# LayerNorm, gated FFN and sliding-window attention on one core: weights in pieces of 128 rows with row halves that swap column blocks, and a first chunk whose first 256 rows go through on their own

## The chip, the core and the metric

The kernel runs on one core of a Trainium2 chip. Its engines work side by side and meet through semaphores only: TensorE (PE; its weight loads are listed apart as PEld), VectorE (DVE), ScalarE (ACT), GpSimd (POOL) and SyncE (SP), the last of which here only starts transfers. Transfers are started from the queues of SP, POOL and, once, ACT, and are carried by 16 DMA engines. Matmul results land in PSUM, eight banks of 512 float32 columns per partition; everything else lies in SBUF, 128 partitions wide.

The metric is device time in microseconds (us), the median of several runs. Before the change: 560.89 us (three runs, 560.74 to 561.54).

## The reference

```python
def reference(x, k_cache, v_cache, wq, wo, B_x, w_gate, w_up, w_down):
    # x (1, 2048, 448); Hq 16 query heads, Hkv 8 key heads, Dh 256; W = 512 last keys
    xn = layernorm(x)                                   # no scale, no bias
    q = (xn @ wq)                                       # 448 x 4096
    p = softmax(q @ k[:, last W].T * Dh**-0.5)          # per head, no mask
    s = (p @ v[:, last W]) @ wo                         # 4096 x 448
    g = silu((gelu(xn @ w_gate) * (xn @ w_up)) @ w_down)  # 448 x 1792 twice, 1792 x 448
    return x + s * g
```

All tensors are bfloat16. `B_x` is not used: both branches take `x`.

## The kernel before

**Recording.** `Rec.op` (L65) records one operation for one engine with the keys that it reads (`r`) and writes (`w`). From the keys it derives what the operation waits for, other engines' operations and transfers. An operation of an engine does not wait for an earlier one of the same engine where the engine's order is enough, and TensorE never waits for itself. `emit` (L98) writes out each engine's list in the recorded order, so the order of the calls in the code is the order in each engine's queue. A wait is placed ahead of the first instruction of an operation, and holds up all that is recorded behind it on that engine.

**Tiling.** The 2048 rows are four chunks (`c`) of 512 rows, each of four tiles (`t`) of 128. The model width of 448 is 7 pieces (`NK`) of 64 (`HP`). Since a piece has 64 rows of contraction, TensorE's 128 rows are used as two halves: one matmul in partitions 0 to 63 and one in 64 to 127 run side by side, each writing its own PSUM bank. `xnT` holds the transposed normalized rows, each piece twice, in both halves of the partitions. In `wgu` the gate weights lie in the lower half and the up weights in the upper half; in `wq` the even heads lie in the lower half and the odd heads in the upper one.

**Start.** `x0` loads the four tiles of chunk 0 on SP's queue, then come the gate and up weights in four slices (`load_gu`, cut at blocks 2, 6 and 10), the rows of chunk 1, `wd`, and the rows of chunks 2 and 3. Chunk 0 is normalized by VectorE (`ln_stats`, `ln_norm`; ScalarE gives the square root), two tiles at a time, and transposed on TensorE (`ln_tr`, 14 matmuls per tile); ScalarE and VectorE copy two tiles each from PSUM. `warm` runs 12 matmuls on zeros before that.

**FFN.** For each chunk, `gate_up(c, f)` runs over 14 blocks (`f`) of 128 FFN columns: 14 matmuls of 512 columns in 7 pairs, gate into bank `s`, up into bank `s + 1`, where the bank pair rotates over three (banks 0 to 5). ScalarE applies GELU to the gate bank (L374), VectorE multiplies it with the up bank (L376) into `actT`. While this goes on, `ln_later` and `ln_later2` normalize the next chunk's tiles: statistics on VectorE, reciprocal square root on POOL (L345, L347), two normalized copies on VectorE (L294), and a transposing transfer on SP's queue (L236). For chunk 0 this begins at block 4 (`lead`), for the others at block 1. `down` (L382) multiplies `actT` with `wd`, four tiles of 14 matmuls of 448 columns, in banks 6 and 7. `load_piece` sends off `wq`, `V` and `wo` in pieces on POOL's queue between these steps.

**Attention.** The last chunk's `down` is not run at its place but cut up as filling (`fill`) for the first slots of attention. The main loop runs over 64 heads-times-chunks (`i`) and four row tiles (`t`), one slot each: `scores` (L420) in bank 4 or 5, exponential on ScalarE (L424) into one of nine buffers `pr`, division on VectorE (L426, L427), transposing transfer into `pT`; `values` (L440) of an earlier head in every second slot, copied out by VectorE (L446); half of an output projection (L460) in each odd slot from `i` = 6. After the values of slot (`i`, 0), with `i` = 3, 7, 11 and so on, `q_burst` computes the queries of the next four heads: four parts of 7 pairs (L406), each copied out by ScalarE over two banks (L410), in bank pairs 0 and 2 by turns; the first burst, after the FFN, uses 4, 0, 2, 0.

Of the kernel before, what the change touches and what calls it, by code (L numbers as in the profile page):

```python
# [11 lines left out]
P = 128  # L12
# [10 lines left out]
class Rec:  # L23
# [41 lines left out]
    def op(self, eng, fn, r=(), w=(), dma=False, after=(), lane=None):  # L65
# [17 lines left out]
        for d, raw in deps:  # L83
            if d.eng == eng and not d.dma and not dma and (eng == "tensor" or not raw and eng != "gpsimd"):
                continue
            d.inc = d.waited = True
            o.deps.append(d)
# [54 lines left out]
def bass_recurrent_scan__sliding_block_cached__geglu_ffn__prompt_kernel(nc, A_x, A_k, A_v, A_wq, A_wo, B_x, B_wg, B_wu, B_wd, out):  # L142
# [6 lines left out]
    QC, TPC, HP = 512, 4, 64  # L149
    NQC = S // QC  # L150
    NT = NQC * TPC
    NK = D // HP
    NF, NJ, NE = F // P, W // P, Dh // P
    assert S % QC == 0 and D % HP == 0 and NE == 2 and NJ == 4 and Hq == 2 * Hkv and Hq % 4 == 0 and NF % 2 == 0
# [4 lines left out]
    with es:  # L159
# [20 lines left out]
        xnT, _ = sb("xnT", [P, NQC, NK, QC], BF16)  # L180
# [3 lines left out]
        wq, _ = sb("wq", [P, NK, Hkv, Dh], BF16)  # L184
        wo, _ = sb("wo", [P, Hq * NE, D], BF16)
        gu_at = off[0]
        wgu, x_at = sb("wgu", [P, NK, F], BF16)
        x4, _ = sb("x4", [P, NT, D], BF16)
        NX = 4
        xn2, d_at = sb("xn2", [P, NX, NK, 2, HP], BF16)  # L190
        wd, _ = sb("wd", [P, NF, D], BF16)
        actT, hb_at = sb("actT", [P, NF, QC], BF16)
        NHB = 4
        hb, ffn_end = sb("hb", [P, NHB, QC], BF16)

# [9 lines left out]
        while at + 2 * W <= d_at:  # L205
            t_, at = sb("pr%d" % len(pr), [P, W], BF16, at)
            pr.append(t_)
        at = hb_at
        while at + 2 * W <= ffn_end:
            t_, at = sb("pr%d" % len(pr), [P, W], BF16, at)  # L210
            pr.append(t_)
# [27 lines left out]
        dve(lambda e: e.memset(actT[:, NF - 1, :], 0.0), w=[("actT", NF - 1)])  # L239
# [9 lines left out]
        wg_v = B_wg.rearrange("(k p) f -> p k f", p=HP)  # L249
        wu_v = B_wu.rearrange("(k p) f -> p k f", p=HP)  # L250
        cuts = [0, 2, 6, 10, NF]
        fslice = {f: s for s in range(4) for f in range(cuts[s], cuts[s + 1])}

        def load_gu(s):
            a, b = cuts[s] * P, cuts[s + 1] * P
            dma("sync", wgu[0:HP, :, a:b], wg_v[:, :, a:b], w=[("wgu", 0, s)])
            dma("sync", wgu[HP:P, :, a:b], wu_v[:, :, a:b], w=[("wgu", 1, s)])
# [6 lines left out]
        for sl in range(4):  # L264
# [4 lines left out]
        for c in range(2, NQC):  # L269
# [5 lines left out]
        wq_v = A_wq.rearrange("(k p) (g two m) -> p k g two m", p=HP, two=2, m=Dh)  # L275
        pieces = [(wq[lo * HP:(lo + 1) * HP, k, :, :], wq_v[:, k, :, lo, :], ("wq", lo, k))
                  for k in range(NK) for lo in range(2)]
# [312 lines left out]
```

## Time and profile before

| what | value |
|---|---|
| median of three runs | 560.89 us |
| the profiled execution | 561.18 us |
| its span, first to last instruction | 559.4 us |
| granted TensorE clock, mean | 1.000 |
| chunk 0 gate and up, first to last matmul | 9.26 to 30.98 us |
| gate and up of one later chunk, by the chain of waits | 21.26 us |
| `down` of one chunk, by the chain of waits | 10.70 us |
| first query burst; the later ones | 6.04 us; 6.15 us |
| one period of four heads with its burst (251.15 to 277.27) | 26.12 us |
| up weights of slice 0 / 1: issue, to landing | 3.36, 4.3 us / 4.70, 7.8 us |
| `wq` pieces, issue to landing, shortest / median / longest | 3.5 / 4.3 / 6.7 us |

How to read it: busy time of an engine is a share of the span; "idle before, releaser" at the end of a group says how long the engine stood still before these instructions and what ended it. A line such as `9.26 3.20 PE L370 ... x28` in the timeline gives start, length, engine, line of the code and how many instructions are merged. The chain of waits is the work that ended last, followed back from the end of the program. In a table by stretches, each engine has its busy time and number of instructions, and the last three columns are the granted clock, the busy share of the DMA engines and GB/s.

### The profile page before, as it was taken

How to read it: one execution, taken by the hardware profiler on the slowest of the kernel's cores; microseconds unless marked ns; L12 is line 12 of the kernel's file. 1: busy time of each engine (PE TensorE's matmuls, PEld its weight loads, DVE VectorE, ACT ScalarE, POOL GpSimd, SP SyncE). 2: the span in 40 equal slices, each digit the busy share in tenths (PEclk: the TensorE clock that was granted, in tenths of full speed). 3: DMA queues.
4: the chain of work that ended last, by engine and by line, in shares of the span. 5: the costliest groups of instructions: out<-in, count | busy, mean ns of one | idle time of the engine just before them, and what ended most of it. 6: DMA issues, size and time to landing. Idle time of an engine off the chain costs nothing.

```text
span 559.4 us, 9865 instructions
## 1 busy us (share of the span) xinstructions
PE 549.0 (98%) x3499; PEld 257.2 (46%) x3532; DVE 322.9 (58%) x835; ACT 296.1 (53%) x673; POOL 90.1 (16%) x125
## 2 busy tenths in 40 slices
PE   7999999999999999999999999999999999999997
PEld 3544444444444444444444444444444444444445
DVE  5636446143464847474846657484747484755674
ACT  4324233247655565556565656656565656565641
POOL 0232323200000111013501101232100021400023
PEclk9999999999999999999999999999999999999999
DMA  8994746972453435353664344445535353645352
GB/s 193 276 191 86 138 102 136 247 137 65 94 85 68 97 64 99 69 91 64 143 98 94 73 86 71 81 84 137 101 67 99 63 95 71 147 79 101 70 92 52
DMA packets 169552, 58.83 MB, mean 105 GB/s; under 512 B 160160, under 2 KB 166432, under 8 KB 169504
## 3 DMA queue, kind: packets, MB, share of 16 engines
q1 hardware_dynamic: 166208, 45.50, 44.2%
q0 software_dynamic: 3152, 12.65, 8.9%
q8 instruction: 28, 0.46, 0.4%
q14 instruction: 20, 0.16, 0.1%
q10 hardware_dynamic: 144, 0.06, 0.0%
HBM read 17.92 MB, written 1.84 MB: 35 GB/s over the span
## 4 chain that ended last, share of the span: by engine, by line
PE 95%; DMA 1%; DVE 1%; issue 1%; SPq 1%; ACT 0%
PE ps L440 20%; PE ps L420 19%; PE ps L406 18%; PE ps L460 16%; PE ps L370 15%; PE ps L382 8%; DMA wgu<-in_B_w_up_dram 1%; SPq L233 1%; DVE tmp L469 0%; DVE ofin L471 0%; DVE pr L427 0%; DVE oT L446 0%; DVE rden L426 0%; ACT pr L424 0%
## 5 line engine op out<-in xcount | busy, mean ns | idle before, releaser
L424 ACT ACTIVATE pr<-ps 128x512 bf16<-128x512 f32 x256 | 152.8, 597 | 116.6 <-PE ps L420 112.5
L420 PE MATMUL ps<-kT,qT 128*128 128x512 bf16 x481 | 145.4, 379 | 3.3 <-issue 2.5
L440 PE MATMUL ps<-pT,V 128*128 128x512 bf16 x510 | 130.8, 379 | 0.6 <-DVE rden L426 0.4
L426 DVE RECIPROCAL rden<-den 128x1 f32<-128x1 f32 x256 | 41.5, 162 | 152.4 <-ACT pr L424 134.3
L460 PE MATMUL ps<-wo,oT 128*128 128x448 bf16 (+1 forms) x536 | 116.3, 344 | 0.0
L427 DVE TENSOR_SCALAR pr<-pr,rden 128x512 bf16<-128x512 bf16 x256 | 106.4, 416 | 9.0
L406 PE MATMUL ps<-xnT,wq 64*128 64x512 bf16 x896 | 99.5, 376 | 0.0
L410 ACT ACTIVATE qT<-ps 128x1024 bf16<-128x1024 f32 x64 | 65.5, 1024 | 49.8 <-PE ps L406 49.8
L370 PE MATMUL ps<-xnT,wgu 64*128 64x512 bf16 x784 | 85.5, 376 | 1.0 <-ACT xnT L322 0.8
L446 DVE CAST oT<-ps 128x512 bf16<-128x512 f32 x124 | 84.6, 682 | 0.6 <-PE ps L440 0.5
L440 PEld LDWEIGHTS ps<-pT,V 128*128 128x128 bf16 x512 | 49.9, 98 | 60.8 <-issue 1.2
L460 PEld LDWEIGHTS ps<-wo,oT 128*128 128x128 bf16 x536 | 52.3, 98 | 51.1
L420 PEld LDWEIGHTS ps<-kT,qT 128*128 128x128 bf16 x512 | 48.5, 98 | 57.1 <-issue 7.3
L376 DVE TENSOR_TENSOR actT<-ps,hb 128x512 bf16<-128x512 f32 x56 | 38.1, 685 | 57.5 <-ACT hb L374 55.7
L406 PEld LDWEIGHTS ps<-xnT,wq 64*128 64x128 bf16 x896 | 42.4, 94 | 55.9 <-DVE acc L481 4.2
L374 ACT ACTIVATE hb<-ps 128x512 bf16<-128x512 f32 x56 | 33.4, 597 | 51.8 <-PE ps L370 51.8
L370 PEld LDWEIGHTS ps<-xnT,wgu 64*128 64x128 bf16 x784 | 39.2, 94 | 46.5 <-issue 2.5
L424 ACT ACTIVATION_READ_ACCUMULATOR pr<-ps 128x1 f32 x256 | 49.9, 195 | 0.0
L500 POOL TENSOR_SCALAR tmp<-tmp 128x448 f32<-128x448 f32 x16 | 9.1, 572 | 233.9 <-ACT tmp L499 233.9
L382 PE MATMUL ps<-wd,actT 128*128 128x448 bf16 x224 | 46.2, 353 | 0.1
L485 POOL TENSOR_TENSOR tmp<-acc,gy 128x448 f32<-128x448 f32 x16 | 16.6, 1035 | 123.2 <-DVE acc L481 123.2
L382 PEld LDWEIGHTS ps<-wd,actT 128*128 128x128 bf16 x224 | 21.7, 98 | 22.2 <-issue 1.3
(43 smaller groups left out, 171.7 us busy)
## 6 DMA issues: line engine op xcount, KB each, us to landing
pT<-pr SPq DMA_TRANSPOSE x256, 2.4
wq<-in_A_wq_dram POOLq DMA_DIRECT2D x14, 256.0 KB, 4.3
wo<-in_A_wo_dram POOLq DMA_DIRECT2D x4, 896.0 KB, 10.1
V<-in_A_v_cache_dram POOLq DMA_DIRECT2D x4, 512.0 KB, 5.8
xr<-in_A_x_dram POOLq DMA_DIRECT2D x4, 448.0 KB, 4.8
wd<-in_B_w_down_dram SPq DMA_DIRECT2D x1, 1568.0 KB, 17.6
wgu<-in_B_w_gate_dram SPq DMA_DIRECT2D x3, 448.0 KB, 10.3
wgu<-in_B_w_up_dram SPq DMA_DIRECT2D x3, 448.0 KB, 11.8
```

The lines of the kernel that those rows point to most:

```text
L370: ins = e.matmul(bank(b), lhsT=wgu[lo:lo + HP, k, f * P:(f + 1) * P], rhs=xnT[lo:lo + HP, c, k, :], start=k == 0, stop=k == NK - 1)
L376: dve(lambda e: e.tensor_tensor(actT[:, f, :], bank(s + 1), hb[:, n % NHB, :], ALU.mult), r=[("ps", s + 1), ("hb", n % NHB)], w=[("actT", f)])
L382: pe(lambda e, f=f: e.matmul(bank(b, D), lhsT=actT[:, f, t * P:(t + 1) * P], rhs=wd[:, f, :], start=f == 0, stop=f == NF - 1), r=[("actT", ...
L406: ins = e.matmul(bank(b), lhsT=wq[lo:lo + HP, k, h0 // 2 + hp, e_ * P:(e_ + 1) * P], rhs=xnT[lo:lo + HP, c, k, :], start=k == 0, stop=k == ...
L410: act(lambda e, e_=e_, s=s, i=i: e.activation(qT[:, i:i + 2, e_, :], psum[:, s * 512:(s + 2) * 512].rearrange("p (a q) -> p a q", a=2), AC ...
L420: ins = e.matmul(bank(b), lhsT=qT[:, i % 6, k, t * P:(t + 1) * P], rhs=kT[:, g, k, :], start=k == 0, stop=k == NE - 1)
L424: act(lambda e: e.activation(pr[s][:, :], bank(b), ACT.Exp, scale=scale, accum_out=den[:, s:s + 1]), r=[("ps", b)], w=[("pr%d" % s,), ("de ...
L426: dve(lambda e: e.reciprocal(rden[:, s:s + 1], den[:, s:s + 1]), r=[("den", s)], w=[("rden", s)])
L427: dve(lambda e: e.tensor_scalar(pr[s][:, :], pr[s][:, :], rden[:, s:s + 1], None, op0=ALU.mult), r=[("pr%d" % s,), ("rden", s)], w=[("pr%d ...
L440: ins = e.matmul(bank(b), lhsT=V[:, j, g, e_ * P:(e_ + 1) * P], rhs=pT[:, i % NPT, j, :], start=j == 0, stop=j == NJ - 1)
L446: dve(lambda e: e.tensor_copy(dst, bank(b)), r=[("ps", b)], w=[key])
L460: ins = e.matmul(bank(b, D)[:, lo:hi], lhsT=oT[G % 2][:, idx, t * P:(t + 1) * P], rhs=wo[:, h0 * NE + idx, lo:hi], start=idx == 0, stop=id ...
```

## The change

The width of 448 is now three pieces (`KF`) of 128 rows and one corner of 64. Weights of gate, up and query lie in SBUF as pieces of 128 rows (`wg`, `wu`, `wq`), the corner apart (`wg6`, `wu6`, `wq6`: lower half for even column blocks, upper half for odd ones). `xnT` holds three pieces once, and the 64-row corner twice. A block `f` is now two column blocks of 128 of the same weight, gate for even `f` and up for odd `f`. `two_blocks` computes it in two phases: in phase 0 the lower row half contributes to the first column block and the upper half to the second, with the corner; in phase 1 they swap, without the corner. Since both phases write the same banks from different row halves, phase 1 waits for phase 0 by a semaphore of TensorE itself (`hard`). Phase 0 of the next block is put between the two. GELU and the product work on two banks, 1024 columns, at once.

The first three blocks of chunk 0 are run for rows 0 to 255 first, with the transposes of tiles 2 and 3 in between, and for rows 256 to 511 afterwards. The corner weights of blocks 0 to 3 are loaded on POOL's queue at the start, the others there too, after a matmul of block 0. In the query bursts the bank pair rotates over 0, 2 and 4. In slot 1 after a burst the output projection goes before the scores; `down` of the last chunk has other slots, and `pr` 12 buffers.

```diff
-    def op(self, eng, fn, r=(), w=(), dma=False, after=(), lane=None):
+    def op(self, eng, fn, r=(), w=(), dma=False, after=(), lane=None, hard=()):
...
+        for d in hard:
+            d.inc = d.waited = True
+            o.deps.append(d)
...
-        cuts = [0, 2, 6, 10, NF]
-        fslice = {f: s for s in range(4) for f in range(cuts[s], cuts[s + 1])}
+        cuts = [0, 2, 4, NF2]
+        jslice = {j: s for s in range(3) for j in range(cuts[s], cuts[s + 1])}
 
         def load_gu(s):
-            a, b = cuts[s] * P, cuts[s + 1] * P
-            dma("sync", wgu[0:HP, :, a:b], wg_v[:, :, a:b], w=[("wgu", 0, s)])
-            dma("sync", wgu[HP:P, :, a:b], wu_v[:, :, a:b], w=[("wgu", 1, s)])
+            a, b = cuts[s] * 2 * P, cuts[s + 1] * 2 * P
+            for w, _, name, src, _ in w_gu:
+                dma("sync", w[:, :, a:b], src[:, :, a:b], w=[(name, s)])
+
+        def load_gu6(a, b, after=()):
+            for _, w6, name, _, src in w_gu:
+                for h in range(2):
+                    dma("gpsimd", w6[h * HP:(h + 1) * HP, a:b, :], src[h, :, a:b, :],
+                        w=[(name + "6", h, a > 0)], after=after)
...
+        load_gu6(0, 2)
+        for sl in range(3):
             load_gu(sl)
...
-        def ln_norm(t, copies=2):
+        def ln_norm(t, twice=True):
             s = t % NX
-            for o in range(copies):
...
+            for lo, a in ((0, 0), (D, D - HP))[:1 + twice]:
+                dve(lambda e, lo=lo, a=a: e.tensor_scalar(
+                    xn2[:, s, lo:lo + D - a], x4[:, t, a:D], mv[:, t, 0:1], rstd[:, t:t + 1],
...
+        warm(38)
+        for t in range(2):
             ln_stats(t)
+            ln_std(t)
+        for t in range(2):
+            ln_first(t)
             ln_tr(t)
+        warm(4)
+        ln_copy(0)
+        ln_stats(2)
+        ln_copy(1)
+        ln_std(2)
+        ln_stats(3)
+        ln_std(3)
+        act(lambda e: e.activation(small[:, 3:4], small[:, 0:1], ACT.Gelu_apprx_tanh), r=[("eps",)], w=[("warm2",)])
+        for t in range(2, TPC):
+            ln_first(t)
...
+        def two_blocks(ph, c, s, cols, w, w6, keys, q0=0, q1=QC):
+            def run(e):
+                for k in range(KF + 1 - ph):
+                    for lo in (0, HP):
+                        m = (lo > 0) ^ ph
+                        lhsT = w[lo:lo + HP, k, cols[m]:cols[m] + P] if k < KF else w6[lo:lo + HP, :]
+                        ins = e.matmul(bank(s + m)[:, q0:q1], lhsT=lhsT, rhs=xnT[lo:lo + HP, c, k, q0:q1],
+                                       start=ph == 0 and k == 0, stop=ph == 1 and k == KF - 1)
+                return ins
+            hard = [phase0[s]] if ph else []
+            phase0[s] = pe(run, r=xn(c)[q0 // P:q1 // P] + keys, w=[("ps", s), ("ps", s + 1)], hard=hard)
...
+        def gate_up(c, f, ph, q0=0, q1=QC):
+            j, up = divmod(f, 2)
             n = c * NF + f
-            s = 2 * (n % NGB)
...
+            s, h = 2 * (n % NGB), (n // 2) % NHB
+            w, w6, name = w_gu[up][:3]
+            keys = [(name, jslice[j])] + ([] if ph else [(name + "6", a, j >= 2) for a in range(2)])
+            two_blocks(ph, c, s, (2 * j * P, (2 * j + 1) * P), w, w6[:, j, :], keys, q0, q1)
+            if ph == 0 or q1 < QC:
+                return
+            two = psum[:, s * 512:(s + 2) * 512].rearrange("p (a q) -> p a q", a=2)
+            if up:
+                dve(lambda e: e.tensor_tensor(actT[:, 2 * j:2 * j + 2, :], two, hb[:, h, :, :], ALU.mult),
...
+                act(lambda e: e.activation(hb[:, h, :, :], two, ACT.Gelu_apprx_tanh),
...
+                s, i, h = 2 * (n % 3), (4 * G + 2 * hp) % 6, h0 + 2 * hp
...
+            for n in range(5):
+                if n < 4:
+                    part(n, 0)
+                if n:
+                    part(n - 1, 1)
...
+            done = 0
+            if c == 0:
+                done = NGB
+                for f in range(NGB + 1):
+                    if f < NGB:
+                        gate_up(0, f, 0, 0, QC // 2)
+                    if f:
+                        if f > 1:
+                            ln_tr(f)
+                            ln_copy(f)
+                        gate_up(0, f - 1, 1, 0, QC // 2)
+            for f in range(NF + 1):
+                if f < NF:
+                    gate_up(c, f, 0, QC // 2 if f < done else 0)
+                if f:
+                    gate_up(c, f - 1, 1, QC // 2 if f - 1 < done else 0)
                 if c + 1 < NQC and lead <= f < lead + 2 * TPC:
-                    t, half = divmod(f - lead, 2)
-                    (ln_later2 if half else ln_later)((c + 1) * TPC + t)
+                    t, part = divmod(f - lead, 2)
+                    (ln_later2 if part else ln_later)((c + 1) * TPC + t)
                 if f >= 9 and f % 2:
                     load_piece()
+                if c == 0 and f == 1:
+                    load_gu6(2, NF2, after=[R.ops["tensor"][-1]])
...
-        for d, slots in ((0, range(0, 4)), (1, range(4, 12)), (2, range(16, 20)), (3, range(20, 24))):
+        for d, slots in ((0, range(0, 4)), (1, range(4, 12)), (2, range(12, 16)), (3, range(16, 20))):
...
             for t in range(TPC):
-                scores(i, t)
-                if 4 * i + t in fill:
-                    down(NQC - 1, *fill[4 * i + t])
+                late = t == 1 and i % 4 == 3
+                if not late:
+                    scores(i, t)
...
+                if late:
+                    scores(i, t)
                 if t == 0 and i % 4 == 3 and i + 1 < NI:
                     q_burst(i // 4 + 1)
+                if 4 * i + t in fill:
+                    down(NQC - 1, *fill[4 * i + t])
```

## The prediction

> **What bounds the kernel now.** I read the page first: span, busy shares, then the groups of instructions.
>
> ```profile
> span 559.4 us, 9865 instructions
> ...
> PE 549.0 (98%) x3499; PEld 257.2 (46%) x3532; DVE 322.9 (58%) x835; ACT 296.1 (53%) x673; POOL 90.1 (16%) x125
> ...
> L410 ACT ACTIVATE qT<-ps 128x1024 bf16<-128x1024 f32 x64 | 65.5, 1024 | 49.8 <-PE ps L406 49.8
> L370 PE MATMUL ps<-xnT,wgu 64*128 64x512 bf16 x784 | 85.5, 376 | 1.0 <-ACT xnT L322 0.8
> ...
> L376 DVE TENSOR_TENSOR actT<-ps,hb 128x512 bf16<-128x512 f32 x56 | 38.1, 685 | 57.5 <-ACT hb L374 55.7
> ```
>
> TensorE is the bound from its first gate matmul to the tail: the projections at L370 idle 1.0 us in 784 matmuls. Only fewer TensorE slots, an earlier start, or a new hole can move the time. The chain of waits gives a slot: a chunk's 196 gate/up matmuls, two at a time in the row halves, take 21.26 us, 0.217 a pair, so 1.52 for a block's 7 pairs.
>
> The timeline of the first 30 us shows the start.
>
> ```profile
> 6.47 2.02 PE L316 MATMUL ps<-ident,xn 128*64 128x128 bf16 x56 [1.09 <-DVE xn L294]
> ...
> 7.77 1.39 DVE L324 COPY xnT<-ps 128x896 bf16<-128x896 bf16 x2
> ...
> 9.26 3.20 PE L370 MATMUL ps<-xnT,wgu 64*128 64x512 bf16 x28 [0.77 <-ACT xnT L322]
> ...
> 12.67 17.66 PE L370 MATMUL ps<-xnT,wgu 64*128 64x512 bf16 x162 [0.22 <-DMA wgu<-in_B_w_up_dram]
> ```
>
> Gate work begins at 9.26, waits 0.22 for the second weight slice, and then has no hole until it ends at 30.98.
>
> **TensorE slots.** None goes. A double block takes 4 pairs in phase 0 and 3 in phase 1: 7, as now. So gains can come from the start alone, and the rest is a search for holes. The own-semaphore wait (`hard`) ahead of each phase 1 costs nothing: between a phase 0 and its phase 1 lie 7 other pairs (1.52 us), in a query burst at least 3 (0.65), in the half-width part 4 half ones (0.46), and a result is visible 0.22 after its slot (first query group 277.20 + 1.51, its copy below at 278.93). Without that cover each of the 123 waits would cost about 0.3.
>
> ```profile
> 277.20 6.22 PE L406 MATMUL ps<-xnT,wq 64*128 64x512 bf16 x56
> ...
> 278.93 1.02 ACT L410 ACTIVATE qT<-ps 128x1024 bf16<-128x1024 f32 x1 [1.80 <-PE ps L406]
> ```
>
> **The start: -1.1.** Tiles 0 and 1 are normalized alone. From the rows of this timeline: second aggregate ends 4.37; reciprocal 0.14 and normalize 0.46 twice put the second tile at 5.5; five transposes (0.3) by 5.9, visible 6.1; VectorE then has stats and aggregate of tile 2 until 6.3 and copies 512 elements in 0.42 (0.62 for 896). First half-width gate block: 6.85. The two weight sides of slice 0 are 786 KB instead of 459, but with 128 destination partitions. Two stretches of one us tell the rate: 17 to 18 us moves 64-partition weights, 25 to 26 the 128-partition `wd`.
>
> ```profile
> 17.00:18.00 1.00, 1.00 (x12) 0.55 (x10) 0.30 (x1) 0.58 (x1) 0.00 (x0) 1.00 1.16 216
> ...
> 25.00:26.00 1.00, 1.00 (x12) 0.54 (x10) 1.00 (x2) 0.57 (x1) 0.00 (x0) 1.00 1.12 353
> ```
>
> Last column GB/s. x's first four tiles land by 4.5 (issues plus their 2.4), so at 353 the up side lands near 7.2, just when its first block wants it; at 216 it is 2.5 us later (a rival). Blocks 0 to 2 over 256 rows are 21 half pairs; a half pair costs between 0.108 (half a slot) and 0.192 (at the tail 48 matmuls of 224 columns of L460 take 4.6 us, 0.096 each with its load, and two make a pair); nearer the first, 0.115. So 15 half pairs reach 8.6; a change of the array's mode (0.16, the hole after each query burst), tile 2's transposes (0.3), a change back, 3 half pairs: 9.5; again a change and tile 3's transposes: 9.95; visible 10.15, copied 10.57, the last 3 half pairs beneath; the second row half starts near 10.7. From there 21 half pairs (2.4) and 77 full pairs (16.7) end at 29.8, if nothing else waits: 1.1 to 1.2 before 30.98. Of the 2.4 us between 6.85 and 9.26 more than half is spent on the changes and on tile 3. Ends: -2.4, all kept, and -0.3.
>
> **The late corner weights: +3.2.** The 64-row corner of blocks 4 to 13 goes out on POOL's queue only after block 0's phase 1 of the second row half. From there to block 4's phase 0, which needs the first two of these four transfers, are only 4+3 half pairs, 4 full, 3 half: 2.0 us. No transfer on that queue has been so quick.
>
> ```profile
> wq<-in_A_wq_dram POOLq DMA_DIRECT2D x14, 256.0 KB, 4.3
> ...
> V<-in_A_v_cache_dram POOLq DMA_DIRECT2D x4, 512.0 KB, 5.8
> ```
>
> A transfer here is 80 KB in 320 runs of 256 B (a wq piece: 512 runs of 512 B). The second issue leaves 0.2 + 0.7 after the block; landing between 3.0 (the wq minimum 3.5, less for the bytes) and 5.4 (the first wq piece, amid other transfers, as here amid x, slice 2 and wd). I take the median 4.3: 5.2 against 2.0 leaves 3.2; ends 1.9 to 4.3. It absorbs another hole: block 3 reuses block 0's banks after only 0.8 us of half pairs, while GELU needs 0.22 + 1.02 + 0.11, so 0.56 would be lost anyway. Behind the wait in TensorE's queue stand all later blocks, and ScalarE and VectorE wait for them.
>
> The Trainium skill (DMA: Bandwidth & Descriptors, Specifications) puts the line rate at 512 B and more per transfer run; these are 256 B. An estimate that counts each run as one of 512 B makes it 160 KB, still under a wq piece, so by the rule too the sum would keep its 3.2; no run here shows a 256 B run on that queue.
>
> **LayerNorm in chunk 0: +1.7.** VectorE's product now covers 1024 columns: from 224, 448 and 512 columns (0.38, 0.62, 0.685 us) 1.05 ns each, so 1.22 (ends 1.07, 1.37). Order in VectorE's queue with `lead` 4: product of block 3, stats, aggregate, normalize, 64-column normalize, product of 5. Between aggregate and normalize it waits for POOL with nothing in between; before, a product stood there.
>
> ```profile
> 18.73 0.62 DVE L288 BATCH_NORM_STATS2 stats<-x 128x6 f32<-128x448 bf16 x1
> ...
> 19.38 0.18 DVE L289 BATCH_NORM_AGGREGATE mv<-stats 128x2 f32<-128x6 f32 x1
> ...
> 19.65 0.22 POOL L345 TENSOR_SCALAR std<-mv 128x1 f32<-128x1 f32 x1 [18.13 <-DVE mv L289]
> 19.96 0.57 POOL L347 TENSOR_TENSOR rstd<-std,small 128x1 f32<-128x1 f32 x1
> ...
> 20.63 0.92 DVE L294 TENSOR_SCALAR xn<-x,mv,rstd 128x448 bf16<-128x448 bf16 x2 [0.31 <-POOL rstd L347]
> ```
>
> Product start to stats start 1.14, stats to normalize 1.90 (18.73 to 20.63), normalize 0.42 and 0.13 (a 128x1 reciprocal; at most another 0.42): 3.59 a round. TensorE's own round of two blocks is 3.04, and block f+3's phase 0 waits for the product of f. So 0.55 is lost at each of blocks 8, 10, 12: 1.7; ends 1.4 to 2.4. Block 13's product follows without loss. In chunks 1 and 2 `lead` is 1, a product stands over POOL's answer, and the round is 2.5: no loss.
>
> **Bank reuse in the other chunks: +0.6.** Product: 0.20 visible + 1.22 + 0.10 to the next matmul = 1.54 against a cover of 7 pairs, 1.51. About 0.04 at blocks 1, 3, 5, 7, 9 of three chunks. Ends 0 and 1.5. GELU (1024 columns, 1.02 like L410) needs 1.35: covered.
>
> **First query burst: +0.7.** Its first part now takes banks 0 and 1, block 12's. GELU of 12 frees them 1.35 after that block, and only block 13's phase 1 (0.65) lies between. Before, banks 4 and 5 were taken first. The other bursts: banks 4 and 5, the scores' own, are new to them; the copy frees them 6.75 after the burst's start, the output projection put before the scores (0.76) covers until 6.97; without it 0.6 would be lost 15 times. Down blocks moved from slots 16-23 to 12-19, the larger probability pool, 512- instead of 896-column transposes and fewer GELU and product instructions lie beside TensorE: 0, within 0.3.
>
> **Sum:** -1.1 + 3.2 + 1.7 + 0.6 + 0.7 = +5.1. The profiled execution took 561.18 (span 559.4 and 1.8 around it): 566.3. It stood 0.3 above the median of the three runs, 560.89, so I say 566.0. The ends sum to +1.6 and +8.6 (the burst's 0.7 as it is); all lows or all highs at once are unlikely: 563 to 569 is this case's own range.
>
> **A closing clock.** Every stretch of this trace has a granted clock of 1.00, and no hole of TensorE after 10 us is over 0.5. The corner hole is near 3. The Trainium skill (TensorE: Matmul & The Clock Gate, Why this matters for your kernels) warns of idle gaps over about 3 us, after which the clock halves; an estimate by its window is 1.7 us more, 567.7. No run here shows it, and I leave it out.
>
> **Rivals.**
> - Faster, 0.10: the start keeps its whole 2.4 us. Its place is the first row half: the changes of mode cost nothing and tile 3 is there in time; the corner transfers land within their 2.0 us and POOL's answer is hidden. Then -2.4 + 0.56 + 0.7 = -1.1: 559.8, and 559.2 if block 3's hole closes too. For it: `wd`'s 353 GB/s and the 0.22 wait for weights that would go. Against it: no transfer of weights on POOL's queue was under 3.5. It is not faster once a corner lands over 2.6 after its block, where the hole passes 0.56.
> - Corner in time, the rest as worked, 0.22: 3.2 shrinks to block 3's 0.56, so 563.4; with nothing for the bank reuse and 1.4 for LayerNorm 562.5, and a start of -1.6 makes it 562.0.
> - Weights at 216 GB/s, 0.12: the up side of slice 0 comes 2.5 us later and stops the first row half; 568.5. Against it: the 216 belongs to 64-partition pieces.
> - The row halves gain nothing because half pairs are bound by weight loads, 0.06: 42 x 0.077 = 3.2 more, 569.2.
> - Forecast, 0.50.
>
> A measurement tells 0.2% (1.1 us) from no change. Faster 0.10; same 0.10 (the low part of the corner-in-time case); slower 0.80. Range 561.0 to 569.8: below it lie the faster rival and a little of the next, above it the tail of the last two, 0.2 in all.
>
> **What would show it.** First gate matmul near 7; a hole of TensorE near 14 to 17 us ended by a `wg6` transfer; in chunk 0 three holes of 0.5 ended by L376's successor; the first query burst 0.7 late; chunks 1 to 3 at 21.3 to 21.6. I am wrong if chunk 0's gate work ends before 31.

## The result and the profile after

The changed kernel takes 574.89 us (median of four runs, 573.92 to 575.62) against 561.02 for the kernel before in the same runs: a ratio of 1.0248, 95% interval 1.0232 to 1.0264. The direction of the forecast is right, its size is not: +5.1 was worked out, +13.9 came between the medians, and 574.89 lies outside the range. Medians here leave out executions whose clock was low over the whole program; for E1, E4 and E5 below that leaves three, and their traces are not read. In the profiled execution (573.92, the fastest of the four) the difference can be read by spans: 572.1 less 559.4 is 12.7 us. The account below explains these 12.7; why the median lies 1.0 higher than this execution is said at E5.

The page of the changed kernel, its span and busy times and the groups that answer to those of before (columns as explained above):

```profile
span 572.1 us, 9790 instructions
...
PE 555.3 (97%) x3535; PEld 260.2 (45%) x3568; DVE 315.0 (55%) x809; ACT 289.3 (51%) x648; POOL 93.7 (16%) x133
...
L427 DVE TENSOR_TENSOR actT<-ps,hb 128x1024 bf16<-128x1024 f32 x28 | 34.2, 1223 | 72.0 <-PE ps L406 64.2
...
L406 PE MATMUL ps<-xnT,wg 64*128 64x512 bf16 (+1 forms) x420 | 50.5, 372 | 6.5 <-DMA wg<-in_B_w_gate_dram 5.1
```

TensorE's busy time has grown by 6.3 although it has 36 more instructions only, so some of its matmuls ran slower; and the gate blocks waited 6.5 us (the up blocks, in a row of their own, 2.2), where gate and up together waited 1.0 before. VectorE's product takes 1.22, as forecast.

The chain of waits from 42 to 137 us shows that chunks 1 to 3 are untouched: 21.26 for the 196 gate and up matmuls of chunks 1 and 2, as before, and 20.63 for the 190 of chunk 3 that stand in the chain, which is the same pace.

```profile
41.96 10.70 PE ps L436 x56
52.66 21.26 PE ps L406 x196
73.92 10.70 PE ps L436 x56
84.62 21.26 PE ps L406 x196
...
116.57 20.63 PE ps L406 x190
```

It also gives the first difference: chunk 0's gate and up work ends at 41.96 instead of 30.98, 10.98 of the 12.7. TensorE's timeline of chunk 0:

```profile
6.80 0.61 PE L406 MATMUL ps<-xnT,wg 64*128 64x256 bf16 x8 [0.24 <-DVE xnT L348]
9.26 1.04 PE L406 MATMUL ps<-xnT,wu 64*128 64x256 bf16 x8 [1.85 <-DMA wu<-in_B_w_up_dram]
10.07 1.72 PE L406 MATMUL ps<-xnT,wg 64*128 64x256 bf16 x14
...
13.98 0.61 PE L406 MATMUL ps<-xnT,wg 64*128 64x256 bf16 x8 [0.18 <-DVE xnT L348]
...
14.85 0.94 PE L406 MATMUL ps<-xnT,wg 64*128 64x256 bf16 x14
...
16.48 1.04 PE L406 MATMUL ps<-xnT,wu 64*128 64x512 bf16 x8 [0.35 <-ACT hb L430]
...
22.94 1.89 PE L406 MATMUL ps<-xnT,wg 64*128 64x512 bf16 x8 [5.10 <-DMA wg<-in_B_w_gate_dram]
...
31.00 1.04 PE L406 MATMUL ps<-xnT,wg 64*128 64x512 bf16 x8 [0.29 <-DVE actT L427]
```

The first gate matmul starts at 6.80, 2.46 earlier than before. Then there are two holes that a transfer ends: 1.85 before the first up block and 5.10 before block 4. After each, the same matmuls take about twice as long: 14 half-width ones 1.72 at 10.07 but 0.94 at 14.85, eight full ones 1.89 at 22.94 but 1.04 at 16.48. The table by stretches says why; the third column from the right is the granted clock:

```profile
9.00:10.00 1.00, 0.74 (x8) 0.65 (x10) 0.00 (x0) 0.28 (x2) 0.00 (x0) 0.53 1.11 393
10.00:12.00 2.00, 2.00 (x21) 1.31 (x17) 0.00 (x0) 0.00 (x0) 0.00 (x0) 0.50 1.02 374
12.00:14.00 2.00, 1.82 (x24) 0.89 (x22) 0.42 (x1) 0.60 (x1) 0.00 (x0) 0.88 1.09 373
...
22.80:26.20 3.40, 3.26 (x16) 1.39 (x18) 0.05 (x1) 0.00 (x0) 0.00 (x0) 0.51 0.02 8
```

What was lost to the clock is (1 - clock) times the stretch: 0.47 + 1.00 + 0.24 = 1.7 after the first hole, 0.49 x 3.40 = 1.7 after the second. The last column shows data arriving at 373 to 393 GB/s in these stretches, no slower than the 353 of the forecast. Which transfers were late is in the chain of waits:

```profile
3.76 5.37 DMA wu<-in_B_w_up_dram
...
16.34 6.46 DMA wg<-in_B_w_gate_dram
```

Both are corners on POOL's queue: 32 KB that took 5.37, and 80 KB that took 6.46.

### The profile page after: what moved, and what is told of

It reads as the page before. It is cut to its first block, busy times and chain, and to the rows that moved or that the text cites. A ratio compares the mean times of both kernels' runs of the same rounds, so it can differ in the third digit from the quotient of the medians.

```text
span 572.1 us, 9790 instructions
## 1 busy us (share of the span) xinstructions
PE 555.3 (97%) x3535; PEld 260.2 (45%) x3568; DVE 315.0 (55%) x809; ACT 289.3 (51%) x648; POOL 93.7 (16%) x133
## 4 chain that ended last, share of the span: by engine, by line
PE 92%; DVE 3%; DMA 2%; issue 1%; POOL 1%; ACT 1%; DVEq 0%; POOLq 0%
PE ps L406 30%; PE ps L496 19%; PE ps L476 19%; PE ps L516 16%; PE ps L436 7%; DMA wg<-in_B_w_gate_dram 1%; DVE actT L427 1%; DMA wu<-in_B_w_up_dram 1%; DVE tmp L525 0%; DVE ofin L527 0%; POOL wg L242 0%; POOL rstd L384 0%; DVE stats L312 0%; DVE pr L483 0%; DVE xn L318 0%
## 5 line engine op out<-in xcount | busy, mean ns | idle before, releaser
L476 PE MATMUL ps<-kT,qT 128*128 128x512 bf16 x480 | 142.6, 379 | 2.4 <-ACT qT L460 0.8
L460 ACT ACTIVATE qT<-ps 128x1024 bf16<-128x1024 f32 x64 | 63.8, 1022 | 57.1 <-PE ps L406 55.5
L516 PEld LDWEIGHTS ps<-wo,oT 128*128 128x128 bf16 x536 | 51.1, 98 | 53.9 <-issue 5.9
L476 PEld LDWEIGHTS ps<-kT,qT 128*128 128x128 bf16 x512 | 49.9, 98 | 54.2 <-issue 1.2
L427 DVE TENSOR_TENSOR actT<-ps,hb 128x1024 bf16<-128x1024 f32 x28 | 34.2, 1223 | 72.0 <-PE ps L406 64.2
L430 ACT ACTIVATE hb<-ps 128x1024 bf16<-128x1024 f32 x28 | 28.6, 1023 | 63.9 <-PE ps L406 63.9
L406 PE MATMUL ps<-xnT,wg 64*128 64x512 bf16 (+1 forms) x420 | 50.5, 372 | 6.5 <-DMA wg<-in_B_w_gate_dram 5.1
L406 PE MATMUL ps<-xnT,wu 64*128 64x512 bf16 (+1 forms) x406 | 49.3, 376 | 2.2 <-DMA wu<-in_B_w_up_dram 1.9
L406 PEld LDWEIGHTS ps<-xnT,wg 64*128 64x128 bf16 x420 | 19.6, 96 | 31.5 <-issue 7.4
```

Of the source, the lines that this page charges most:

```text
L406: ins = e.matmul(bank(s + m)[:, q0:q1], lhsT=lhsT, rhs=xnT[lo:lo + HP, c, k, q0:q1], start=ph == 0 and k == 0, stop=ph == 1 and k == KF - 1)
L427: dve(lambda e: e.tensor_tensor(actT[:, 2 * j:2 * j + 2, :], two, hb[:, h, :, :], ALU.mult), r=[("ps", s), ("ps", s + 1), ("hb", h)], w=[( ...
L430: act(lambda e: e.activation(hb[:, h, :, :], two, ACT.Gelu_apprx_tanh), r=[("ps", s), ("ps", s + 1)], w=[("hb", h)])
L460: act(lambda e: e.activation(qT[:, i:i + 2, e_, :], psum[:, s * 512:(s + 2) * 512].rearrange("p (a q) -> p a q", a=2), ACT.Copy), r=[("ps" ...
L476: ins = e.matmul(bank(b), lhsT=qT[:, i % 6, k, t * P:(t + 1) * P], rhs=kT[:, g, k, :], start=k == 0, stop=k == NE - 1)
L516: ins = e.matmul(bank(b, D)[:, lo:hi], lhsT=oT[G % 2][:, idx, t * P:(t + 1) * P], rhs=wo[:, h0 * NE + idx, lo:hi], start=idx == 0, stop=id ...
```

## The account, term by term

| term | forecast | measured in the spans |
|---|---|---|
| the start, up to the second row half | -1.1 | +2.3 |
| the late corners, with block 3's hole | +3.2 | +5.45 (5.10 + 0.35) |
| clock after that hole | left out | +1.65 |
| LayerNorm in chunk 0 | +1.7 | +1.56 |
| bank reuse in chunks 1 to 3 | +0.6 | 0 |
| first query burst | +0.7 | +1.73 |
| rest of attention | 0 | -0.27 + 0.31 |
| sum | +5.1 | +12.7 |

The start's +2.3 is what is left of chunk 0's 10.98 after the other terms of that chunk. It misses the forecast by 3.4, and 1.85 (first hole) + 1.7 (clock) are 3.55 of this. LayerNorm: the products (L427) of blocks 3, 5, 7, 9 and 11 start about 3.56 apart where TensorE's round is 3.04, and TensorE waits for them ahead of blocks 8, 10 and 12, three times 0.52. The burst is shown at E4.

## The experiments

| | edit | us | ratio to before, 95% |
|---|---|---|---|
| changed kernel | | 574.9 | 1.0248 (1.0232 to 1.0264) |
| E1 | late corners sent at the start | 567.9 | 1.0121 (1.0104 to 1.0138) |
| E2 | `wd` and later rows sent after block 4 | 568.8 | 1.0138 (1.0123 to 1.0153) |
| E3 | `lead` 5 | 573.5 | 1.0227 (1.0208 to 1.0245) |
| E4 | first burst takes banks 6, 4, 0, 2 | 572.9 | 1.0211 (1.0194 to 1.0228) |
| E5 | idle matmuls in both holes | 572.2 | 1.0197 (1.0178 to 1.0216) |
| E6 | first corners on ScalarE's queue | 573.7 | 1.0221 (1.0203 to 1.0239) |
| E7 | no row halves at the front | 573.7 | 1.0223 (1.0206 to 1.0241) |
| E8 | E1 + E3 + E4 + E6 | 565.7 | 1.0080 (1.0065 to 1.0095) |
| E9 | small first slice, late corners behind slice 1, E3, E4, E6 | 562.9 | 1.0033 (1.0020 to 1.0046) |
| E10 | no row halves, late corners behind slice 1, E3, E4, 30 idle matmuls | 561.1 | 1.0007 (0.9998 to 1.0016) |
| E11 | E3 + E4 + E5 | 569.2 | 1.0146 (1.0132 to 1.0159) |

**E1: is the late corner the big term?**

```diff
         load_gu6(0, 2)
+        load_gu6(2, NF2)
...
-                if c == 0 and f == 1:
-                    load_gu6(2, NF2, after=[R.ops["tensor"][-1]])
```

> All corner weights go out at the start on POOL's queue, those of blocks 4 to 13 right behind the first four and without a wait. Theory (the corners are late because they are sent late): they land before block 4 wants them near 17.6 us, the 5.1 us hole goes and with it the 1.6 us that the halved clock costs after it: about 568.2 against 574.9. Rival (the block would wait for its main weight slices or for something else as long): under 2 us is gained, 573 or more. Four more transfers in flight may hold up the up corner of blocks 0 to 3 and stretch the first hole by up to 1 us.

It takes 7.0 us off, close to the second hole and the clock that falls with it (5.10 + 1.65 = 6.75): half of the loss between the medians goes when the late corners are sent early. That it is this hole that went is read from the size of the gain; E8, which sends them as early, shows no wait at block 4 in its trace.

**E2: why does an 80 KB corner take over 6 us?** The bulk on SP's queue behind the weights is sent later; the corner stays where the change put it.

```diff
-        dma("sync", wd[:, :, :], B_wd.rearrange("(f p) d -> p f d", p=P), w=[("wd",)])
-        for c in range(2, NQC):
-            load_x(c)
...
+                if c == 0 and f == 5:
+                    dma("sync", wd[:, :, :], B_wd.rearrange("(f p) d -> p f d", p=P), w=[("wd",)], after=[R.ops["tensor"][-1]])
+                    for c2 in range(2, NQC):
+                        load_x(c2)
```

> wd and the rows of chunks 2 and 3 are sent only after block 4 of chunk 0, so that no bulk is in flight when the late corner transfers go out near 15.7 us; these stay where they are. Theory (a corner transfer of 80 KB takes 6.0 to 6.5 us because it shares the DMA engines with the bulk on SP's queue): it lands in about 3, like the very first one at 1.7 us (2.9), the second hole shrinks from 5.1 to about 1.7, and the clock stays or falls: 570 to 571.5. Rival (256 B runs or POOL's own work make it slow, with or without bulk): 6 us to landing as before and 574 to 575.

The transfers of this kernel from 10 to 28 us (KB each, median us from issue to landing), and its timeline and stretch at block 4:

```profile
wg<-in_B_w_gate_dram POOLq DMA_DIRECT2D x2, 80.0 KB, 2.5
wu<-in_B_w_up_dram POOLq DMA_DIRECT2D x2, 80.0 KB, 2.6
```

```profile
20.02 1.04 PE L403 MATMUL ps<-xnT,wg 64*128 64x512 bf16 x8 [1.17 <-DMA wg<-in_B_w_gate_dram]
```

```profile
20.00:24.00 4.00, 3.98 (x38) 2.02 (x40) 1.94 (x3) 0.74 (x1) 0.18 (x1) 1.00 0.08 21
```

E2 takes 6.1 us off the median, more than expected. The same transfer, with the same runs of 256 B on the same queue, lands in 2.5 us. What made it 6 is the company of `wd` (1568 KB) and the later rows (448 KB each) on SP's queue, not its shape and not POOL. The Trainium skill (DMA: Bandwidth & Descriptors, Anatomy of one DMA — SWDGE (gpsimd) path) gives a fit for one transfer on this path, about 2.0 us plus its bytes at 436 GB/s; an estimate by it for 80 KB is 2.2. The 2.5 measured here is near it; the estimate says nothing of the 6.0 to 6.5 beside other traffic. The hole is 1.17 and the clock stays at 1.00 after it.

**E3: LayerNorm's round.**

```diff
-            lead = 4 if c == 0 else 1
+            lead = 5 if c == 0 else 1
```

> The next chunk's LayerNorm starts at block 5 instead of 4 in chunk 0, so that VectorE has a product between aggregate and normalize, as in chunks 1 and 2. Theory (VectorE's wait for POOL's answer in the open lengthens its round from 3.04 to 3.56): the rounds go back to 3.04 to 3.1, three holes of 0.5 vanish: -1.6, 573.3. Rival (TensorE's wait there is for the longer product itself, not for LayerNorm): no change, rounds of 3.5.

The medians differ by 1.4, near the 1.56 that the trace gave; the two intervals overlap, so the time alone does not show it. In the chain of waits of this kernel chunk 0 is now one piece after block 4's corner:

```profile
16.23 6.52 DMA wg<-in_B_w_gate_dram
22.75 0.14 issue
22.89 18.36 PE ps L406 x146
```

VectorE has left the chain: with the normalization begun one block later, a product stands between aggregate and normalize, and POOL's answer comes while it runs.

**E4: the first query burst.** In the changed kernel it looks so (timeline; the last line is the first `scores`):

```profile
138.31 1.04 PE L406 MATMUL ps<-xnT,wq 64*128 64x512 bf16 x8 [0.47 <-ACT hb L430]
139.63 5.35 PE L406 MATMUL ps<-xnT,wq 64*128 64x512 bf16 x48 [0.29 <-DVE actT L427]
145.76 0.38 PE L476 MATMUL ps<-kT,qT 128*128 128x512 bf16 x1 [0.78 <-ACT qT L460]
```

Three waits, of which the prediction had only the first. The second part wants banks 2 and 3, block 13's, which VectorE's product frees only after GELU of block 12 has been made (the product needs both). And the first scores want bank 4 back from the third part's copy.

```diff
-                s, i, h = 2 * (n % 3), (4 * G + 2 * hp) % 6, h0 + 2 * hp
+                s, i, h = 2 * (n % 3) if G else (6, 4, 0, 2)[n], (4 * G + 2 * hp) % 6, h0 + 2 * hp
```

> The first query burst takes bank pairs 6, 4, 0, 2 instead of 0, 2, 4, 0; all else as changed. Theory (the first burst loses 0.48 to GELU of block 12, 0.45 to the product of block 13, which itself waits for that GELU, and 0.6 at the first scores, which wait for bank 4): all three go, -1.5 to -1.7, 573.2. Rival (only the one wait that was forecast, 0.7, belongs to the banks): -0.7, 574.2.

It takes 2.0 us off (572.4 to 573.6 in its executions), as expected within its interval. E11 below has the same edit: there the burst is one piece, with 0.16 before the scores.

```profile
134.79 6.21 PE L414 MATMUL ps<-xnT,wq 64*128 64x512 bf16 x56
141.16 0.38 PE L484 MATMUL ps<-kT,qT 128*128 128x512 bf16 x1 [0.16 <-issue]
```

From the last up matmuls to the first scores it is 7.02 there (134.14 to 141.16), 8.74 in the changed kernel (137.02 to 145.76): 1.7 less.

**E5: what does the clock cost by itself?** Idle matmuls on data that nothing reads fill the holes, without closing them.

```diff
+        def idle(n):
+            def run(e):
+                for _ in range(n):
+                    ins = e.matmul(bank(7, P), lhsT=actT[:, NF - 1, 0:P], rhs=actT[:, NF - 1, 0:P], start=True, stop=True)
+                return ins
+            pe(run, r=[("actT", NF - 1)], w=[("ps", 7)])
...
+                    if f == 1:
+                        idle(30)
...
+                if c == 0 and f == 4:
+                    idle(80)
```

> Nothing is sent earlier; TensorE runs 30 and 80 idle matmuls of 128 columns on zeros (bank 7, results unused) in the two holes of chunk 0, ahead of block 1 and of block 4. They fit into the holes. Theory (each hole is followed by some 3.4 us at a granted clock of 0.5, 1.6 us lost each time): the clock stays at 1.00 through both, -3.2, 571.7. Rival (the clock does not follow the holes, or the lower clock hides behind waits): 574 to 575, or more if the idle matmuls outlast the transfers.

2.7 us come back between the medians although more work is done. The medians hide something here. The four executions of the changed kernel took 573.92, 574.23, 575.55 and 575.62 us at a mean granted clock of 0.994, 0.991, 0.988 and 0.988; over the span this is some 3.4, 5.1, 6.9 and 6.9 us of clock lost, or two, three, four and four stretches of 3.4 us at half clock. The three executions of E5 were granted 1.000 and lie within 0.12 us. So the median of the changed kernel holds more closings than the profiled execution, and gains between medians can hold some of that. Against the profiled execution, where two closings cost 3.4 by the table of stretches, E5 is only 1.7 less. Where a part of the rest goes can be seen in E11, which has the same idle matmuls: at full clock TensorE comes to block 5 before its up corner has landed.

```profile
24.66 1.04 PE L414 MATMUL ps<-xnT,wu 64*128 64x512 bf16 x8 [1.20 <-DMA wu<-in_B_w_up_dram]
```

**E6: the first hole.** The corners of blocks 0 to 3 leave from ScalarE's queue (`load_gu6` takes the queue as an argument).

```diff
+        load_gu6(0, 2, q="scalar")
         act(lambda e: e.activation(small[:, 2:3], small[:, 0:1], ACT.Sqrt), r=[("eps",)], w=[("warm",)])
-        load_gu6(0, 2)
```

> Only the corner weights of blocks 0 to 3 move: to ScalarE's queue, at the very start, ahead of the bulk; the late ones stay on POOL's. Theory (the first hole is the wait for the up corner, issued at 3.8 and landed at 9.1): it lands by 5, the first hole shrinks from 1.85 to 0.4 or less and the clock stays up: -1.5 to -3. The late corner is then sent 3 us earlier, when more bulk is in flight: if it needs some 6 to 7 us there, the second hole stays 5 and the time is 572 to 573.4; if it starves until the bulk is through near 22 us (rival), the second hole takes up all that was won: 574 to 575.

```profile
8.01 0.61 PE L406 MATMUL ps<-xnT,wg 64*128 64x256 bf16 x8 [0.78 <-DVE stats L312]
8.97 0.61 PE L406 MATMUL ps<-xnT,wu 64*128 64x256 bf16 x8 [0.35 <-DMA wu<-in_B_w_up_dram]
...
12.29 0.61 PE L406 MATMUL ps<-xnT,wg 64*128 64x256 bf16 x8 [0.18 <-DVE xnT L348]
...
21.28 1.89 PE L406 MATMUL ps<-xnT,wg 64*128 64x512 bf16 x8 [5.13 <-DMA wg<-in_B_w_gate_dram]
```

The first hole shrinks to 0.35, the matmuls after it are at full speed, and the second row half starts 1.7 earlier. But the first gate block moves from 6.80 to 8.01: x's four tiles now land 2.7 us after their issue instead of 2.1, beside four corners that take 2.7 to 3.5. And the second hole is as long as ever, because its transfer is issued earlier and takes as long. The gain stays at 1.2, a little under what was expected and within the overlap of the two intervals. In this trace the clock after the second hole also costs more:

```profile
19.74:26.56 6.82, 5.28 (x26) 2.28 (x28) 1.94 (x3) 0.00 (x0) 0.01 (x1) 0.50 0.52 149
```

It falls at 19.74, before block 4 begins at 21.28, and stays at half for twice as long as in the changed kernel; TensorE is busy 5.28 us of it, against 3.26 in the stretch from 22.80 to 26.20 there.

**E7: the row halves taken away.**

```diff
-                done = NGB
-                for f in range(NGB + 1):
-                    ...
+                for t in range(2, TPC):
+                    ln_tr(t)
+                    ln_copy(t)
```

> The first three blocks are not split into row halves: tiles 2 and 3 are transposed and copied first, then every block runs with 512 columns; all else as changed. Theory (the split starts early but only runs into the corner that is not there): the first matmul comes near 9.5, no first hole and no halved clock before the second one; the late corner, sent near 12, still stops block 4 for some 4 us: 569.5 to 571.5. Rival (the split brings the 1.1 us that was forecast for it): 576.

The gain of 1.2 is smaller than expected, and within the overlap of the two intervals. The clock closes here too, after an idle stretch of only 1.44 us between the transposes (6.3 to 7.75). These are the stretches from 7 to 13:

```profile
7.00:9.00 2.00, 1.25 (x10) 0.67 (x10) 1.09 (x6) 1.72 (x4) 0.00 (x0) 0.74 1.10 321
9.00:13.00 4.00, 3.42 (x20) 1.21 (x20) 0.42 (x1) 0.55 (x2) 0.00 (x0) 0.50 1.06 380
```

So the early row half as the change has it is worth nothing: it begins 2.80 earlier than E7 (6.80 against 9.60) and loses that again to its hole and the clock.

**E8: all four remedies at once.** E3 and E4 as above, and for the corners:

```diff
+        load_gu6(0, 2, q="scalar")
+        load_gu6(2, NF2)
         act(lambda e: e.activation(small[:, 2:3], small[:, 0:1], ACT.Sqrt), r=[("eps",)], w=[("warm",)])
-        load_gu6(0, 2)
...
-                if c == 0 and f == 1:
-                    load_gu6(2, NF2, after=[R.ops["tensor"][-1]])
```

> The changed kernel with its four causes taken away together: first corner weights on ScalarE's queue at the start, the late ones on POOL's queue at the start, LayerNorm from block 5, bank pairs 6, 4, 0, 2 in the first burst. Theory (the four account for the loss): 574.9 less 3.0, 6.7, 1.5 and 1.6, so 561 to 562.5. Rival (the row exchange itself, its own semaphore waits or the wider products cost something throughout): 564 or more.

The expectation fails by 3 us or more: 565.7. The number falls on the rival's side, but the trace puts the loss at the start and not throughout. Chunk 0 now has no hole at block 4, but begins at 9.66, and the span is 4.7 over the kernel before, about what `down` of chunk 0 starts later (35.70 against 30.91). Eight small corner transfers at the start share the engines with x's tiles and the first slices: x's tiles land 3.3 us after their issue, where it was 2.1, and the 384 KB pieces of slices 0 and 1 after 7.1 and 7.8, where it was 4.5 and 5.2. The stretches, and behind them the one from 6 to 8 of the changed kernel:

```profile
4.00:6.00 2.00, 1.16 (x15) 0.99 (x12) 1.25 (x6) 1.33 (x4) 0.64 (x1) 1.00 0.87 209
6.00:8.00 2.00, 1.20 (x14) 0.62 (x12) 1.93 (x6) 0.89 (x2) 0.00 (x0) 1.00 1.05 261
8.00:10.00 2.00, 0.34 (x4) 0.34 (x6) 1.01 (x5) 1.78 (x3) 0.00 (x0) 0.51 1.09 260
```

```profile
6.00:8.00 2.00, 1.17 (x15) 0.68 (x14) 1.80 (x7) 1.11 (x4) 0.00 (x0) 1.00 1.11 339
```

From 6 to 8 the DMA engines are nearly as busy as in the changed kernel (1.05 against 1.11) but bring 261 GB/s in place of 339; TensorE waits 2.46 and its clock closes once more. The gains of E1, E3, E4 and E6 do not add, because two of them use the same engines in the same microseconds.

**E9: first slice cut smaller, late corners behind slice 1.** The first corners as in E6, E3 and E4 as above, the line that sent the late corners after block 0 is gone, and:

```diff
-        cuts = [0, 2, 4, NF2]
+        cuts = [0, 1, 3, NF2]
...
             if sl == 1:
+                load_gu6(2, NF2, q="sync")
                 load_x(1)
```

> The changed kernel with its row halves kept, but the first four corner blocks on ScalarE's queue, the four late corner blocks on SyncE's queue behind slice 1 of the bulk (so that they neither share the engines with slice 0 nor stand behind wd), the first slice cut smaller (one pair of blocks instead of three), the transposes five groups ahead and the query burst's pairs in the order 6, 4, 0, 2. Theory (the loss is the time at which small blocks arrive, and the clock lost in the holes that this leaves): first gate matmul at 7 to 8, no hole over 1 us in chunk 0, clock at 1.00 after the first few us, gate work of chunk 0 ends at 29 to 31, time 559 to 561.5. Rival (the start is bound by the number of bytes and small runs, so a smaller slice 0 only moves the wait to slice 1): holes of 1 to 3 us before blocks 2 to 4, gate work ends at 33 or later, 563 to 566.

Neither side is quite met: 562.9. The clock is at 1.00 throughout and block 4 does not wait, but as the rival had it, the wait moves to the next slice:

```profile
7.45 0.61 PE L407 MATMUL ps<-xnT,wg 64*128 64x256 bf16 x8 [0.26 <-ACT std L354]
...
10.18 0.61 PE L407 MATMUL ps<-xnT,wg 64*128 64x256 bf16 x8 [1.35 <-DMA wg<-in_B_w_gate_dram]
```

`down` of chunk 0 starts at 32.42, 1.5 later than before.

**E10: the swap of column blocks alone, well fed.**

```diff
-        warm(4)
+        warm(30)
...
             if sl == 1:
+                load_gu6(2, NF2, q="sync")
                 load_x(1)
```

with E3, E4 and E7's edit, and without the line that sent the late corners after block 0.

> The changed kernel without the two row halves in front (the first 256 rows go through as one), the late corner blocks on SyncE's queue behind slice 1, lead of five groups, pairs in the order 6, 4, 0, 2, and 30 idle matmuls between the first transposes and the first gate block to keep TensorE busy there. Theory: first gate matmul at 9.3 to 9.6 with the clock at 1.00, no hole over 1 us after it, gate work ends at about 31, the rest as before: 560.5 to 561.5. If the row exchange itself cost anything beyond arrival times and clock, it would be 563 or more with the same start; if the up corner on POOL's queue still lands late, a hole of 1 to 2 us stands before the first up block and the time is 563 to 565.

```profile
6.33 1.85 PE L328 MATMUL ps<-actT 128*128 128x128 bf16 x30
...
10.01 1.04 PE L407 MATMUL ps<-xnT,wg 64*128 64x512 bf16 x8 [0.83 <-ACT xnT L351]
```

The chain of waits has chunk 0 in one piece:

```profile
10.01 21.32 PE ps L407 x196
```

561.1 against 560.7 (span 559.2 against 559.4), no difference that can be told, and chunk 0 takes 21.32 where a later chunk took 21.26 before. Exchanging row halves, the waits of TensorE on itself, blocks of 1024 columns and the other order of banks cost nothing that shows. The loss was one of arrival times, of the clock and of two orders of work. What the row halves at the front would cost with everything there in time is not shown, since E10 leaves them out; E9, which keeps them, lies 2.3 above the kernel before, with a wait of 1.35 in it.

**E11: do the small terms add?** E5's idle matmuls, and:

```diff
-            lead = 4 if c == 0 else 1
+            lead = 5 if c == 0 else 1
...
-                s, i, h = 2 * (n % 3), (4 * G + 2 * hp) % 6, h0 + 2 * hp
+                s, i, h = 2 * (n % 3) if G else (6, 4, 0, 2)[n], (4 * G + 2 * hp) % 6, h0 + 2 * hp
```

> The changed kernel with the idle matmuls in both holes, the lead of five groups and the pairs in the order 6, 4, 0, 2: three edits that were each tried alone (2.65, 1.4 and 1.65 us). If they are separate terms, they add: 574.9 less 5.7 = 569.2 (568.7 to 569.8), clock at 1.00 through both holes, and what is left over the kernel before is the two holes themselves. If they overlap (the lead only moves work into time that the clock loses), it is 570.5 or more.

569.2, as the sum has it (with E4's 2.0 in place of 1.65 it would be 568.8, also within what the intervals allow). The stretches show the clock at full speed through both holes:

```profile
9.00:12.00 3.00, 2.87 (x45) 2.02 (x41) 0.00 (x0) 0.78 (x2) 0.00 (x0) 1.00 1.06 380
...
18.00:23.00 5.00, 4.45 (x70) 3.75 (x69) 0.00 (x0) 0.00 (x0) 0.00 (x0) 1.00 0.98 270
23.00:26.00 3.00, 1.80 (x20) 0.74 (x16) 1.94 (x3) 0.00 (x0) 0.35 (x2) 1.00 0.06 18
```

What is left of the loss, 8.5, lies in chunk 0, whose `down` starts at 39.02, 8.1 later than before. It is mostly the wait for the corners: 1.9 before the first up block (idle matmuls fill it), 5.2 before block 4, and the 1.20 before block 5 shown at E5.

## Why the prediction was right in direction and wrong in size

- **What bounds the kernel, and the slots:** right. No gate, up or query matmul was added, the chain of chunks 1 to 3 keeps its pace, and E10 shows no cost of the exchange.
- **The start, -1.1:** wrong. Its first gate matmul (6.85 forecast, 6.80 measured), the half pairs (0.77 for seven, so 0.11 each), and the rate of 128-row pieces were right; the up side of slice 0 landed at 7.7 (issued at 3.06, 4.6 to landing) where 7.2 was taken. What failed is that the step counts slice 0's 786 KB and forgets what else block 1 waits for: the corner `wu6` on POOL's queue, fourth of four behind three issues of 0.6 to 0.8, landing at 9.13. The change's own description names these four transfers; the sum has no line for them.
- **The late corner weights, +3.2:** right in mechanism, too small. From the end of the matmul that releases them (15.38) the second transfer lands 7.4 later (22.80), where 5.2 was taken; TensorE's work in between is 2.1, against 2.0 in the forecast; and block 3's hole is absorbed, as forecast: 5.45 comes in two pieces, 0.35 and 5.10. The mis-sized number is the transfer, 4.3 for 6.46. The step names the company ("amid x, slice 2 and wd") and then takes the median of all `wq` pieces. Even its other end, 5.4 for the piece amid other transfers, was short. E2 settles it: 2.5 without that company, 6 or more in it.
- **A closing clock:** "I leave it out" failed. It was worth 3.4 by the stretches; E5 gives 2.7 between medians and 1.7 against the profiled execution. The page (the Trainium skill, TensorE: Matmul & The Clock Gate, Why this matters for your kernels) warned of gaps over about 3 us. The 5.10 hole agrees; but here the clock also closed at a hole of 1.85, at one of 2.46 (E8) and, between sparse transposes, at one of 1.44 (E7), while 1.17 (E2), 1.20 (E11) and 1.35 (E9) did no harm. The measurement decides: a hole well under 3 us can be enough. More on the low clock stands below this list.
- **LayerNorm, +1.7:** right (1.56, and in E3 the wait is gone from the chain). The reading that mattered was which instruction stands between aggregate and normalize in VectorE's queue.
- **Bank reuse, +0.6:** wrong, nothing was lost; the chain shows the pace of before in all three chunks. The 0.04 that was to be missing at each block is below what such a sum of rows can tell.
- **First query burst, +0.7:** too small, 1.73. The step followed the GELU of block 12 to its bank, but not to the product of block 13 that needs its result, nor the rotation on to bank 4, which the scores take next.
- **Rivals:** weights at 216 GB/s and half pairs bound by weight loads fall by the rows above. The case that a corner comes in time falls, and with it the faster one, which needs it. A case in which corners cost more than any earlier row of that queue was not among them, and this is why the range was too narrow: four terms missed upward together (the start by 3.4, the late corner by 2.25, the clock by 1.65, the burst by 1.0). That the direction came out right owes most to the late corner, sound in its mechanism: as forecast it alone outweighed the start's gain.

The low clock does not simply follow a hole. In E3 the first hole ends at 9.51, and the clock falls only after 10.75:

```profile
9.50:10.75 1.25, 1.24 (x22) 1.10 (x22) 0.00 (x0) 0.00 (x0) 0.00 (x0) 1.00 1.02 390
10.78:14.19 3.41, 3.41 (x30) 1.80 (x30) 0.42 (x1) 0.60 (x1) 0.00 (x0) 0.50 1.06 372
21.02:27.85 6.83, 4.96 (x24) 2.09 (x26) 1.75 (x2) 0.00 (x0) 0.00 (x0) 0.50 0.19 47
```

Worked out from stretches of half a microsecond, every low stretch in the traces read lasts about 3.41 or 6.83 us, and where a trace has two they begin a multiple of 3.41 apart: at 9.06 and 22.72 in the changed kernel and 7.98 and 21.63 in E7 (four times 3.41), at 10.78 and 21.02 in E3 (three times). This suggests a fixed beat, so that what a hole costs depends also on where it falls in it. TensorE is busy 3.0 to 6.3 us of these stretches; an estimate from that is 1.5 to 3.1 us lost to one. No run moved a hole alone, so this is not tested.

What stays open: just what in the DMA engines makes a small transfer wait 4 us beside bulk on another queue, and what, within the beat that the low stretches suggest, decides that the clock closes. The runs bound both and do not explain them.

## What to carry to other kernels

List every transfer that the first use of a block needs, small ones too, and price a small transfer by rows that had the same company, not by the median of all rows of its queue. A hole of TensorE can be paid twice, once by its length and once by a stretch at half clock (1.7 us after each of the two holes here, as the account has it), so ask of every hole over one microsecond what the clock does next. And compare the granted clock of single executions before reading a gain of one or two microseconds out of medians. When banks rotate, follow the bank to who frees it, and that instruction to what it needs itself.

## What the runs showed of the hardware that was not expected

- An 80 KB transfer on POOL's queue takes 2.5 us alone (E2) and 6.0 to 6.5 beside large transfers of SP's queue in the changed kernel, and up to 8.05 in E11. In E10, sent on SP's own queue behind slice 1, the medians are 6.4 and 7.0; there it is issued early enough.
- With all eight corner transfers at the start the DMA engines brought 261 GB/s from 6 to 8 us (E8), with four of them 339 (the changed kernel), at nearly the same busy share.
- With 30 matmuls of 128 columns (1.85 us) in the early idle stretch, and 80 (4.64 us) in the second hole of E11, the clock stayed at 1.00 (E10, E11).
- The low clock came in stretches of about 3.41 or 6.83 us, which began up to 1.9 us before a hole ended or 1.3 after it (both in E3).
